# Source one-hots compared in place over their indices, 42 buckets at a time; destination one-hots in a stream of their own

## The chip, the cores and the metric

The kernel runs on one core of one Trainium2 chip. The metric is the device time of one execution in microseconds, as the median of several runs. The core has five engines that matter here: TensorE (PE, with PEld for its weight loads), VectorE (DVE), ScalarE (ACT), GpSimd (POOL) and SyncE (SP), which only issues DMAs in the stage of interest.

## The reference

One GraphSAGE layer over a random graph of N = 12500 nodes with D = 64 features and E = 800000 edges:

```python
nsum = segment_sum(x[src], dst, N)        # add up the features of each node's neighbours
h_neigh = nsum * deg_inv[:, None]
return x @ w_self + h_neigh @ w_neigh
```

`src` and `dst` are uniformly random. The costly part is the gather `x[src]` of 800000 rows and the sum by `dst`.

## The kernel before

Nodes are taken in source blocks of 128 (NB = 98) and destination blocks of 2 x 82 = 164 (NDB = 77). An edge belongs to one of NBID = 77 x 98 = 7546 **buckets** (destination block, source block). The kernel first sorts the edges by bucket, and then computes each bucket with two one-hot matrix products.

*Sorting.* The edges are packed into 32-bit keys, 6250 to a partition, and each partition is sorted by compare-exchange steps on DVE. The sorted runs are cut into three parts (29, 20 and 10 buckets a row), gathered by POOL's indirect DMAs and merged on DVE (`merge_round`, lines 300 to 334). Part 0 is merged before the sums begin; parts 1 and 2 are merged while the sums run, a few DVE steps after every tile, paced by `PACE` (line 52). Decoding a part (`decode_buckets`) writes each bucket's 128 source indices as a row of `sl` in HBM (bf16) and its destination indices into `dlT` in SBUF.

*Summing* (`nodes`, lines 909 to 1055), from about 819 us to 1875 us of the profile. It goes through the buckets in order, in tiles of 8. For each tile:

- `gather` (line 922): for each bucket one matmul on PE (line 932), with the bucket's **source one-hot** (128 x 128, fp16) as weights and the 128 node rows `xh` of its source block as moving data. The result is the gathered features, in `ct` in PSUM (three buffers). One copy of 1024 columns brings them to `xg` in SBUF (six buffers), on ACT (line 942), or on DVE (line 940) in the last part of the stage, for every second tile at which the stock of ready one-hots is nearly down to the next block (line 935).
- `sums` (line 992), two to five tiles later: for each bucket two matmuls of 64 rows (line 1012) with `xg` as weights and the bucket's **destination one-hot** (128 x 82 twice) as moving data, which add into the accumulators of six destination blocks.
- Now and then `extras` and `pick` take edges that did not fit a bucket (lines 955 to 990), and `finish` multiplies with the weights and adds to the output (lines 1070 to 1091).

*The one-hots* come from `one_hots` (line 890), 28 buckets in each step, 270 steps:

- SP issues four DMAs (line 899) that lay the 28 x 128 source indices of the block, broadcast, into all partitions of an index buffer `slb` (three buffers). Each DMA writes every fourth partition.
- DVE compares the buffer with the partition's number into `ohs` (line 901, three buffers): the source one-hots of 28 buckets.
- DVE compares `iota` with the destination indices in `dlT` into `ohd` (line 906, four buffers): the destination one-hots of the same 28 buckets.

`gather` takes a next step of this generator whenever fewer one-hots are ready than the tile needs and 44 more (`AHEAD`, line 66; 36 once parts 1 and 2 are merged). The order of the work is the order of the program: each engine and each DMA queue takes its instructions in the order in which the Python code emits them, and waits at the first whose data or buffer is not free. So DVE's comparisons stand between the merge steps, and SP's loads stand one after another, each waiting until its index buffer is free.

Of the kernel before, what the change touches and what calls it, by code (L numbers as in the profile page):

```python
# [13 lines left out]
BF = mybir.dt.bfloat16  # L14
FH = mybir.dt.float16
I32 = mybir.dt.int32
U32 = mybir.dt.uint32
OP = mybir.AluOpType
# [7 lines left out]
HN = 82  # L26
NDB = -(-N // (2 * HN))
NBID = NDB * NB
# [42 lines left out]
BEHIND = 5e3  # L71
NEARLY = 24
LAG = 4
HELD = 5
OCT = 6
OCTM = 256 // OCT + 1
# [297 lines left out]
class Kernel:  # L374
# [348 lines left out]
    def find_and_gather(self, part, vp):  # L723
# [7 lines left out]
        junk = vp.tile([128, max(n for _, n in WIN.w2[part])], BF, name="junk")  # L731
        for k in range(kpr + LAG):
            if k == 1:
                self.store_rows(part, nc.gpsimd)
            if k < kpr:
                self.count_below(part, k, acc, junk)
            if k >= LAG:
                g = k - LAG
                nc.scalar.activation(ix[:, g:g + 1], acc[:, g:g + 1], AF.Relu, bias=self.c2[part][:, 3, g:g + 1])
# [147 lines left out]
        self.left[part] = (place, s)  # L887
        yield 1

    def one_hots(self, pool):  # L890


        nc = self.nc
        for c in range(0, NBID, 28):
            n = min(28, NBID - c)
            b = pool.tile([128, 28 * 128], BF, name="slb", bufs=3)[:, :n * 128]
            src = self.sl[c:c + n]
            for j in range(4):
                nc.sync.dma_start(b[j::4], bass.AP(tensor=src.tensor, offset=src.offset, ap=[[0, 32], [1, n * 128]]))  # L899
            s = pool.tile([128, 28, 128], FH, name="ohs", bufs=3)[:, :n]  # L900
            nc.vector.tensor_scalar(s.rearrange("p c s -> p (c s)"), b, self.pidx[:, :1], None, op0=OP.is_equal)  # L901
            d = pool.tile([128, 14, HN, 2], FH, name="ohd", bufs=4)[:, :n // 2]
            at = c % TURN
            wide = [128, n // 2, HN, 2]
            ix = self.dlT[:, at:at + n].rearrange("p (c t) -> p c t", t=2)[:, :, None, :].to_broadcast(wide)
            nc.vector.tensor_tensor(d, self.iota[:, None].to_broadcast(wide), ix, op=OP.is_equal)  # L906
            yield [(s[:, j], d[:, j // 2, :, j % 2]) for j in range(n)]

    def nodes(self, pool, aps, mps):


        nc = self.nc
        source = self.one_hots(pool)
        ready = []
        pend = []
        late = []
        done = []
# [4 lines left out]
        def gather(b0, cnt, vector):  # L922

            nonlocal turn
            ct = aps.tile([128, 1024], F32, name="ct", bufs=3)
            ahead = AHEAD - 8 * vector
            while len(ready) < min(cnt + ahead, NBID - b0):
                ready.extend(next(source))
            cols = ready[:cnt]
            del ready[:cnt]  # L930
            for i in reversed(range(cnt)):
                nc.tensor.matmul(ct[:, i * 128:(i + 1) * 128], cols[i][0],  # L932
                                 self.xh[:, (b0 + i) % NB].rearrange("p a f -> p (a f)"), start=True, stop=True)
            xg = pool.tile([128, 1024], FH, name="xg", bufs=6)
            if vector and (len(ready) < min(8 + ahead, NBID - b0 - cnt) or NBID - b0 < 56):
                turn += 1
            else:
                vector = False
            if vector and turn % 2:
                nc.vector.tensor_copy(xg[:, :cnt * 128], ct[:, :cnt * 128])  # L940
            else:
                nc.scalar.activation(xg[:, :cnt * 128], ct[:, :cnt * 128], AF.Copy)  # L942
            return b0, xg, [d for _, d in cols]
# [11 lines left out]
        def pick(b0):  # L955
            if self.picked == len(done) or len([u for u in uses if u[5]]) >= HELD:
                return
            u = next((u for u in uses if not u[5]), None)
            if u and u[1] in self.left and b0 + LEAD >= u[4] * NB:
                _, p, c = u[:3]  # L960
                x = u[5] = pool.tile([128, 128], FH, name="lx", bufs=HELD)
                u[6] = len(done)
                nc.gpsimd.indirect_dma_start(  # L963
                    out=x, out_offset=None, in_=self.xt,
                    in_offset=bass.IndirectOffsetOnAxis(ap=self.left[p][1][:, c:c + 1].bitcast(U32), axis=0))
                self.picked = len(done)

        def spread(u):
            o, p, c, f, e = u[:5]
            u[7] = pool.tile([128, 2, OCT * HN], FH, name="ohl", bufs=HELD)  # L970
            n = slice((f - o * OCT) * HN, (e - o * OCT) * HN)
# [10 lines left out]
        def extras(b0, cnt):  # L982
            o = b0 // (OCT * NB)
            for u in uses[:HELD]:
                if u[5] and not u[7] and len(done) >= u[6] + 10 and b0 + 80 >= (u[4] - 1) * NB:
# [47 lines left out]
        for t, (b0, cnt) in enumerate(tiles):  # L1033
            pend.append(gather(b0, cnt, self.changed))
            if (len(pend) > 5) if self.changed else t % 2:
                while len(pend) > (3 if self.changed else 2):
                    b0 = pend[0][0]
                    if sums(pend.pop(0)):
                        break
                extras(b0, 8)  # L1040
            else:
                pick(b0)
            b0 = tiles[t][0]
            if late and b0 >= late[0][0]:
                if next(late[0][1], self) is self:
                    late.pop(0)
                else:
                    late[0][0] = b0 + 40
            done.append(t)
            yield t  # L1050
# [323 lines left out]
```

## Time and profile before

| what | value |
|---|---|
| median of 3 runs | 1880.74 us (1879.26 to 1881.54) |
| the profiled execution, its time | 1892.56 us |
| the profiled execution, its span | 1890.8 us |
| DVE busy over the span | 1739.8 us (92%) |
| ACT busy | 1125.0 us (59%) |
| PE busy | 969.4 us (51%) |
| POOL busy | 580.3 us (31%) |
| source comparisons, line 901 | 270, 322.9 us on DVE |
| destination comparisons, line 906 | 270, 361.8 us on DVE |
| index loads, line 899 | 1080 DMAs, 224 KB each but the last four |

Times in rows of the profile are in microseconds from the first instruction, unless marked ns. The shares over the whole span mix two very different stages: until about 811 us DVE sorts and PE does nearly nothing; after that all engines work on the sums. Read the stage, not the span. A row of a group has the line, the engine, the operation, what it writes and reads with the shapes, its count, then its busy time and the mean of one, and after a second bar the idle time of the engine ahead of it and who ended it.

### The profile page before, as it was taken

How to read it: one execution, taken by the hardware profiler on the slowest of the kernel's cores; microseconds unless marked ns; L12 is line 12 of the kernel's file. 1: busy time of each engine (PE TensorE's matmuls, PEld its weight loads, DVE VectorE, ACT ScalarE, POOL GpSimd, SP SyncE). 2: the span in 40 equal slices, each digit the busy share in tenths (PEclk: the TensorE clock that was granted, in tenths of full speed). 3: DMA queues.
4: the chain of work that ended last, by engine and by line, in shares of the span. 5: the costliest groups of instructions: out<-in, count | busy, mean ns of one | idle time of the engine just before them, and what ended most of it. 6: DMA issues, size and time to landing. Idle time of an engine off the chain costs nothing.

```text
span 1890.8 us, 54010 instructions
## 1 busy us (share of the span) xinstructions
PE 969.4 (51%) x23335; PEld 850.3 (45%) x23335; DVE 1739.8 (92%) x1728; ACT 1125.0 (59%) x1578; POOL 580.3 (31%) x447
## 2 busy tenths in 40 slices
PE   0042000000000000058878989887888999889996
PEld 0041000000000000047767878776777788678885
DVE  8999999999999999989969999999986999888885
ACT  7281000104001005458979999899898999878875
POOL 2000000045421004404545435473324324432231
PEclk9975555555555555569989999999899999989998
DMA  4353000022001002168969898987797999878884
GB/s 154 70 133 71 0 0 0 37 63 65 14 8 59 22 0 75 51 199 246 285 201 262 274 259 251 294 267 226 217 302 210 275 281 272 274 194 258 262 260 121
DMA packets 176788, 307.77 MB, mean 163 GB/s; under 512 B 127885, under 2 KB 133340, under 8 KB 175772
## 3 DMA queue, kind: packets, MB, share of 16 engines
q1 hardware_dynamic: 98268, 275.58, 44.5%
q0 software_dynamic: 78272, 28.65, 9.5%
q8 instruction: 184, 3.01, 0.6%
q14 instruction: 64, 0.52, 0.1%
HBM read 277.01 MB, written 26.52 MB: 161 GB/s over the span
## 4 chain that ended last, share of the span: by engine, by line
DVE 20%; PE 13%; DMA 11%; issue 9%; ACT 6%; SPq 6%; POOL 1%; DVEq 0%; another core or an unknown queue 0%; POOLq 0%; ACTq 0%
DMA slb<-sl 10%; DVE u L328 7%; PE ct L932 7%; SPq L899 6%; PE acc L1012 5%; ACT xg L942 4%; DVE ohs L901 4%; DVE ohd L906 4%; DVE u L362 2%; DVE u L316 1%; PE po L1079 1%; ACT u L689 0%; PE acc L980 0%; ACT junkb L544 0%; POOL out L1088 0%
## 5 line engine op out<-in xcount | busy, mean ns | idle before, releaser
L942 ACT ACTIVATE xg<-ct 128x1024 f16<-128x1024 f32 x918 | 863.3, 1061 | 124.8 <-PE ct L932 88.3
L932 PE MATMUL ct<-xh,ohs 128*128 128x128 f16 x7546 | 537.9, 224 | 86.7 <-DVE ohs L901 48.9
L932 PEld LDWEIGHTS <-ohs 128*128 128x128 f16 x7546 | 453.2, 100 | 126.3 <-DVE ohs L901 55.4
L328 DVE TENSOR_TENSOR u<-u 128x1512 f32<-128x1512 f32 (+57 forms) x316 | 426.8, 1361 | 13.0 <-ACT u L312 8.3
L1012 PE MATMUL acc<-ohd,xg 64*128 64x82 f16 x15092 | 401.3, 202 | 50.3 <-ACT xg L942 21.3
L963 POOL DMA_INDIRECT lx<-xt,ls x127 | 240.4, 1893 | 458.3 <-PE acc L980 377.3
L1012 PEld LDWEIGHTS <-xg 64*128 64x128 f16 x15092 | 327.9, 97 | 111.1 <-issue 39.7
L901 DVE TENSOR_SCALAR ohs<-slb,pidx 128x3584 f16<-128x3584 bf16 x270 | 322.9, 1196 | 54.2 <-PE ct L932 19.5
L906 DVE TENSOR_TENSOR ohd<-iota,dlT 128x2296 f16<-128x2296 bf16 x270 | 361.8, 1340 | 0.9 <-PE acc L1012 0.9
L500 PE MATMUL stp<-cx,swapa 128*128 128x16 f32 (+1 forms) x12 | 3.1, 335 | 445.9 <-DVE swapa L496 445.9
L500 PEld LDWEIGHTS stp<-cx,swapa 128*128 128x128 f32 x12 | 2.6, 274 | 446.4 <-issue 236.4
L260 DVE TENSOR_TENSOR a<-b 128x1040 f32<-128x1040 f32 (+41 forms) x130 | 194.8, 1539 | 5.2 <-ACT b L262 2.1
L260 DVE TENSOR_TENSOR b<-a 128x1040 f32<-128x1040 f32 (+46 forms) x150 | 194.7, 1346 | 3.4 <-DVE a L260 0.5
L529 POOL DMA_INDIRECT u<-d,ixa x48 | 72.5, 1510 | 402.1 <-ACT junka L517 346.7
L1088 POOL DMA_DIRECT2D out<-o x27 | 100.1, 3835 | 93.4 <-ACT o L1082 76.2
L312 ACT ACTIVATE u<-u 128x256 f32<-128x256 f32 (+14 forms) x60 | 33.0, 623 | 160.4 <-DVE u L316 124.3
L778 PE MATMUL tr<-idb,l 128*128 128x128 bf16 x59 | 7.8, 268 | 188.8 <-ACT l L772 188.8
L262 ACT ACTIVATE b<-a 128x2 f32<-128x2 f32 (+31 forms) x41 | 16.0, 405 | 147.8 <-DVE a L260 131.1
L778 PEld LDWEIGHTS <-l 128*128 128x128 bf16 x59 | 4.4, 116 | 191.2 <-ACT l L772 190.8
L316 DVE TENSOR_TENSOR u<-u 128x2016 f32<-128x2016 f32 (+11 forms) x40 | 62.5, 1574 | 25.5 <-DMA lx<-xt,ls 15.7
L262 ACT ACTIVATE a<-b 128x1 f32<-128x1 f32 (+24 forms) x34 | 8.6, 259 | 119.4 <-DVE b L260 114.7
L556 POOL DMA_INDIRECT u<-da,ixb x24 | 36.5, 1519 | 79.8 <-ACT ixb L504 75.8
(151 smaller groups left out, 821.1 us busy)
## 6 DMA issues: line engine op xcount, KB each, us to landing
slb<-sl SPq DMA_DIRECT2D x1076, 224.0 KB
xt<-xh SPq DMA_DIRECT2D x1, 3136.0 KB
out<-o POOLq DMA_DIRECT2D x25, 123.0 KB
own<-os SPq DMA_DIRECT2D x12, 256.0 KB
out<-os SPq DMA_DIRECT2D x12, 256.0 KB
rd<-dst SPq DMA_DIRECT2D x4, 521.0 KB
rs<-src SPq DMA_DIRECT2D x4, 521.0 KB
lx<-xt,ls POOLq DMA_INDIRECT x127
```

The lines of the kernel that those rows point to most:

```text
L260: nc.vector.tensor_tensor(view(dst, lo + sh, [[st, g], [1, l]]), x, y, op=op)
L316: nc.vector.tensor_tensor(at(oth, to, n), x, y, op=op)
L328: nc.vector.tensor_tensor(to, at(cur, ln + lo, n), at(cur, lo + k, n), op=op)
L529: nc.gpsimd.indirect_dma_start(out=u[:, i * w:(i + 1) * w], out_offset=None, in_=src, in_offset=bass.IndirectOffsetOnAxis(ap=self.start[pa ...
L899: nc.sync.dma_start(b[j::4], bass.AP(tensor=src.tensor, offset=src.offset, ap=[[0, 32], [1, n * 128]]))
L901: nc.vector.tensor_scalar(s.rearrange("p c s -> p (c s)"), b, self.pidx[:, :1], None, op0=OP.is_equal)
L906: nc.vector.tensor_tensor(d, self.iota[:, None].to_broadcast(wide), ix, op=OP.is_equal)
L932: nc.tensor.matmul(ct[:, i * 128:(i + 1) * 128], cols[i][0], self.xh[:, (b0 + i) % NB].rearrange("p a f -> p (a f)"), start=True, stop=True)
L942: nc.scalar.activation(xg[:, :cnt * 128], ct[:, :cnt * 128], AF.Copy)
L963: nc.gpsimd.indirect_dma_start(out=x, out_offset=None, in_=self.xt, in_offset=bass.IndirectOffsetOnAxis(ap=self.left[p][1][:, c:c + 1].bit ...
L1012: nc.tensor.matmul(acc[h][:, db % OCT * HN:(db % OCT + 1) * HN], xg[r, i * 128:(i + 1) * 128], d[r], start=db % OCT == 0 and sb == 0, stop ...
L1088: nc.gpsimd.dma_start(out, o[:n, at], accum_op=OP.add)
```

## The change

`one_hots` is split into two generators.

`source_hots` makes the source one-hots of 42 buckets in each step (`SCH`), 180 steps. It has one kind of buffer, of which there are four: SP's four DMAs load the broadcast indices into it, and DVE's comparison writes the fp16 one-hots over the bf16 indices, element by element. The buffer is free again when PE's matmuls have used its last bucket.

`dest_hots` makes the destination one-hots of 28 buckets in each step (`DCH`), with the same operation and the same four buffers as before.

`gather` keeps two stocks, `ready` for the source and `spare` for the destination one-hots, and steps the generator whose stock is smaller until both hold what the tile needs and `AHEAD` more.

```diff
+SCH = 42
+DCH = 28
...
-    def one_hots(self, pool):
+    def source_hots(self, pool):
         nc = self.nc
-        for c in range(0, NBID, 28):
-            n = min(28, NBID - c)
-            b = pool.tile([128, 28 * 128], BF, name="slb", bufs=3)[:, :n * 128]
+        for c in range(0, NBID, SCH):
+            n = min(SCH, NBID - c)
+            b = pool.tile([128, SCH * 128], BF, name="ohs", bufs=4)[:, :n * 128]
             src = self.sl[c:c + n]
             for j in range(4):
                 nc.sync.dma_start(b[j::4], bass.AP(tensor=src.tensor, offset=src.offset, ap=[[0, 32], [1, n * 128]]))
-            s = pool.tile([128, 28, 128], FH, name="ohs", bufs=3)[:, :n]
-            nc.vector.tensor_scalar(s.rearrange("p c s -> p (c s)"), b, self.pidx[:, :1], None, op0=OP.is_equal)
-            d = pool.tile([128, 14, HN, 2], FH, name="ohd", bufs=4)[:, :n // 2]
+            s = b.bitcast(FH)
+            nc.vector.tensor_scalar(s, b, self.pidx[:, :1], None, op0=OP.is_equal)
+            yield [s[:, j * 128:(j + 1) * 128] for j in range(n)]
+
+    def dest_hots(self, pool):
+        nc = self.nc
+        for c in range(0, NBID, DCH):
+            n = min(DCH, NBID - c)
+            d = pool.tile([128, DCH // 2, HN, 2], FH, name="ohd", bufs=4)[:, :n // 2]
...
             nc.vector.tensor_tensor(d, self.iota[:, None].to_broadcast(wide), ix, op=OP.is_equal)
-            yield [(s[:, j], d[:, j // 2, :, j % 2]) for j in range(n)]
+            yield [d[:, j // 2, :, j % 2] for j in range(n)]
...
-            while len(ready) < min(cnt + ahead, NBID - b0):
-                ready.extend(next(source))
-            cols = ready[:cnt]
+            need = min(cnt + ahead, NBID - b0)
+            while min(len(ready), len(spare)) < need:
+                if len(ready) <= len(spare):
+                    ready.extend(next(sources))
+                else:
+                    spare.extend(next(dests))
+            cols = list(zip(ready[:cnt], spare[:cnt]))
             del ready[:cnt]
+            del spare[:cnt]
```

More of the change, by code (lines that the diff above doesn't have):

```diff
@@ L906, in one_hots @@
             nc.vector.tensor_tensor(d, self.iota[:, None].to_broadcast(wide), ix, op=OP.is_equal)
-            yield [(s[:, j], d[:, j // 2, :, j % 2]) for j in range(n)]
+            yield [d[:, j // 2, :, j % 2] for j in range(n)]
     def nodes(self, pool, aps, mps):
         nc = self.nc
-        source = self.one_hots(pool)
-        ready = []
+        sources, dests = self.source_hots(pool), self.dest_hots(pool)
+        ready, spare = [], []
         pend = []
```

## The prediction

> **What bounds the kernel now.** The change touches one stage, so I first looked for the engine that sets its pace: the view of busy time by stretch, over the summing stage (819 to 1875 us) cut at its quiet places. Columns: length, then busy time and instructions of PE, PEld, DVE, ACT, POOL, then granted clock, DMA share, GB/s.
>
> ```profile
> 819.00:1400.00 581.00, 503.57 (x12464) 440.64 (x12465) 550.68 (x673) 521.87 (x669) 261.53 (x141) 0.95 0.84 255
> ...
> 1460.00:1560.00 100.00, 90.74 (x2384) 79.85 (x2380) 97.61 (x107) 94.35 (x115) 32.28 (x13) 1.00 0.91 281
> 1560.00:1875.00 315.00, 280.43 (x7107) 250.03 (x7103) 270.63 (x330) 261.10 (x328) 102.09 (x62) 0.95 0.83 245
> ```
>
> and over two pieces of it:
>
> ```profile
> 1010.00:1260.00 250.00, 223.41 (x5709) 195.45 (x5707) 248.23 (x268) 232.24 (x293) 125.03 (x57) 0.99 0.88 265
> 1640.00:1875.00 235.00, 207.41 (x5313) 186.75 (x5312) 198.91 (x238) 186.88 (x230) 65.33 (x39) 0.95 0.80 234
> ```
>
> DVE is full in the first and third stretch (95% and 98%; 99% in 1010 to 1260), where it also merges runs. PE and ACT follow at 87 to 94%, so little can be won before they bind. In the last stretch DVE is at 86%, PE at 89%: there PE, not DVE, is nearest to the bound.
>
> Next, the chain of waits in 1000 to 1260, for what releases DVE, and three of its pieces from 1110 on (start, us, what):
>
> ```profile
> by line: DMA slb<-sl 32.4%; SPq L899 13.3%; DVE ohs L901 10.5%; DVE ohd L906 8.7%; issue 8.4%; PE ct L932 8.4%; DVE u L328 7.9%; PE acc L1012 7.0%; ACT xg L942 1.5%; DVE ohl L972 1.0%; PE po L1079 0.7%; PE acc L980 0.6%; DVEq L901 0.4%; ACT
> ...
> 1110.19 6.56 DMA slb<-sl
> ...
> 1118.06 0.45 SPq L899
> ...
> 1120.45 4.86 DMA slb<-sl
> ```
>
> This is a loop: comparing a block frees its index buffer, SP issues four loads into it (1118.06 to 1120.45, 2.4 us), the last lands 4.9 to 6.6 us later, and three blocks on that buffer is compared. It takes 45.7% of that chain, yet the idle time it leaves is small, as the waits of 819 to 1400 (first two rows) and of 1400 to 1875 (the last) show (us, times, longest):
>
> ```profile
> PE ct L932 <- DVE ohs L901: 45.0, 21, 22.1
> ...
> DVE ohs L901 <- DMA slb<-sl: 11.3, 7, 6.3
> ...
> DVE ohs L901 <- DMA slb<-sl: 7.3, 6, 2.2
> ```
>
> So the loop ends just as DVE comes free: DVE and the loop are both near critical, and DVE's own work is the larger.
>
> **The change, part by part.** The 28-bucket comparisons, 270 of them, become 180 of 42 (7546 = 179 x 42 + 28). Only their fixed cost goes. Two timeline rows from mid-stage and two from the end price it (the first number is the start):
>
> ```profile
> 1120.60 1.15 DVE L901 TENSOR_SCALAR ohs<-slb,pidx 128x3584 f16<-128x3584 bf16 x1
> 1121.66 1.35 DVE L906 TENSOR_TENSOR ohd<-iota,dlT 128x2296 f16<-128x2296 bf16 x1
> ...
> 1868.42 0.68 DVE L901 TENSOR_SCALAR ohs<-slb,pidx 128x1792 f16<-128x1792 bf16 x1
> 1869.01 0.75 DVE L906 TENSOR_TENSOR ohd<-iota,dlT 128x1148 f16<-128x1148 bf16 x1
> ```
>
> Durations overlap, so starts are compared: 28 buckets hold DVE 1.06 us, 14 hold it 0.59 us. Fourteen buckets cost 0.47 us, and the fixed part is 2 x 0.59 - 1.06 = 0.12 us. A block of 42 holds it 1.53 us. Before: 269 x 1.06 + 0.59 = 285.7 us; after: 179 x 1.53 + 1.06 = 274.9; saved 10.8 us. Where does it count? Line 901 by stretch (only DVE busy):
>
> ```profile
> 819.00:1400.00 581.00, 174.95 (x147) 0.95 0.84 255
> ...
> 1460.00:1560.00 100.00, 34.93 (x29) 1.00 0.91 281
> ```
>
> Of the 147 + 29 = 176 comparisons in the two full stretches a third goes: 59 x 0.12 = **7.1 us** on the path. The other 3.7 us lie in stretches where PE's matmuls hide them.
>
> [...]
>
> Comparing in place: no row has this operation at its four-elements rate. The nearest are an in-place integer operation and two made alike, one in place and one not:
>
> ```profile
> L761 DVE TENSOR_SCALAR v<-v 128x512 int32<-128x512 int32 x14 | 6.0, 427 | 0.5
> ...
> L453 DVE SCALAR_TENSOR_TENSOR g<-g,a 128x1042 int32<-128x1042 int32 x4 | 5.0, 1246 | 0.1
> L455 DVE SCALAR_TENSOR_TENSOR a<-rs,s 128x1042 int32<-128x1042 int32 x4 | 5.0, 1245 | 0.4
> ```
>
> In place 1246 ns, otherwise 1245: I take zero. The other end is that the operation falls to half rate, 180 x 1.4 us = 252 us more DVE work; a rival below. A gain has no reason: the elements stay the same.
>
> Comparisons held up by POOL: some overlap a POOL write and last twice as long.
>
> ```profile
> 1162.78 4.21 POOL L1088 DMA_DIRECT2D out<-o  x1
> ...
> 1163.42 2.29 DVE L901 TENSOR_SCALAR ohs<-slb,pidx 128x3584 f16<-128x3584 bf16 x1
> ```
>
> ```profile
> L901 DVE TENSOR_SCALAR ohs<-slb,pidx 128x3584 f16<-128x3584 bf16 x269 | 322.3, 1198 | 54.2 <-PE ct L932 19.5 <-DMA slb<-sl 18.6 <-issue 6.4
> ```
>
> The mean of 1198 is 48 ns over the 1.15 us of the undisturbed row above, 13 us in all. Fewer operations may meet POOL less often (a third less, 4.3 us won) or longer ones more often (half more, 6.5 us lost). I take zero, since POOL's work stays as it is.
>
> Buffers and loads: three index and three one-hot buffers of 28 become four shared ones of 42, 168 buckets either way. Loads fall from 1080 to 720, bytes stay, so the DMA engines (84% busy) gain nothing sure. SP now waits for the ct matmuls of the block four before instead of for DVE. Behind that wait stand only the next such loads, and DVE waits for them. With one bucket in about 1.05/8 = 0.131 us (250 us over 5709/24 = 238 tiles), the lead works out so. Before: from one comparison to that three blocks on, 84 buckets, 11.0 us, against 1.06 + 2.4 of issues + 4.86 = 8.3. After: loads start when PE finishes a block, at bucket 42k, for the comparison that stands in the program 44 to 52 buckets ahead of 42(k + 3): 74 to 82 buckets, 9.7 to 10.7 us, against 2.4 + 4.86 = 7.3 if the larger load lands as fast, 2.4 + 7.3 = 9.7 if its landing grows with its bytes. So the loop is met, barely at worst, and a DVE that falls behind now gives the loads more time instead of delaying them. Of the 11.3 us, 6.3 are the start; of the other 5.0 I count half as gone: **2.5 us**, bounds 0 and 5.0.
>
> [...]
>
> The start: PE's first matmul waits for the first block.
>
> ```profile
> 813.31 36.97 SPq L899 DMA_DIRECT2D slb<-sl  x42
> ...
> 819.53 1.15 DVE L901 TENSOR_SCALAR ohs<-slb,pidx 128x3584 f16<-128x3584 bf16 x1 [6.34 <-DMA slb<-sl]
> ```
>
> Of these 6.2 us, 2.3 are issues; the remaining 3.9 grow by 0 to 2, I take 1.5, and the comparison by 0.47: **2.0 us lost**. PE then has 42 buckets where it had 28.
>
> Destination one-hots: same 270 operations, four buffers, only the place in DVE's order differs; nothing. DVE casts of xg:
>
> ```profile
> L940 DVE CAST xg<-ct 128x1024 f16<-128x1024 f32 x32 | 39.0, 1220 | 20.4 <-PE ct L932 18.8 <-ACT o L1082 1.0 <-issue 0.5
> ```
>
> Line 935 picks them when a new source block is near, now every 42 buckets: about ten move to ACT, 11 us of work where ACT has 187 of 235 us; PE covers it, and uncovered it would cost at most those 11. Part 2's rows are now read from bucket 6258 on, not 6272. At 1640, after the part is written, PE still has 5313/24 = 221 tiles, so stands near bucket 5775, some 60 us ahead: nothing.
>
> Sum: -7.1 - 2.5 + 2.0 = **-7.6 us**. The profiled execution took 1892.56 us (span 1890.8) and would take 1885.0; the median of the runs, 1880.74, was 11.8 lower, and I carry the difference over: **1873 us**. Its own range, from no loop gain and the slow start (-4.6) to all 5.0, a quick start and fewer collisions (-16), is 1865 to 1877.
>
> **Rivals.** *The loop was the real bound.* For it: its 45.7% of the chain. Against it: DVE is idle so little. Then PE's waits for one-hots beyond the start, 45.0 - 22.1 = 22.9 us, go: -22.9 + 2.0, **1860 us**. *PE and ACT take over at once.* For it: ACT at 94% in the fullest stretch and PE at 91%. Then the 7.1 falls away, and 2.0 lost stands against 2.5: **1880 us**. *The loads come late (slower).* They now wait for PE, and a load like that of 6.56 us, half as large again, lands after 2.4 + 9.8 = 12.2 us, 2.0 beyond the mean lead of 10.2; DVE stands, and with it the destination one-hots, merges and casts queued behind. It decides where landing exceeds some 7.8 us after the last issue. The 12 waits after the start (6 in each half of the stage) each grow by 2.0; the six of the first half, where DVE is full, cost 12.0, against 7.1 won and 2.0 lost: +6.9, **1888 us**. *In place is slower:* DVE gets 252 us; its idle time in the three stretches, 30 + 2 + 44 = 76 us, takes some, so about +170, **2050 us**.
>
> **How the numbers follow.** Forecast 0.45, loop 0.15, no change 0.20, late loads 0.17, slow in place 0.03. A measurement tells 0.2%, 3.8 us: faster 0.45 + 0.15 = 0.60, same 0.20, slower 0.17 + 0.03 = 0.20. The range reaches from just below the loop case, 1858, to just beyond the late loads, 1889; outside are slow in place and the far halves of these two, about 0.18.
>
> **What would show it.** Right: line 901's successor 180 times, start to start 1.53 us; DVE busy 11 us lower; 720 loads; SP waiting for PE; waits of the comparison for slb under 12 us after the start. Wrong: comparisons near 3 us (in place), slb waits above 25 us (late loads), or DVE idle growing by as much as it was relieved (PE and ACT bind).

## The result, and the profile after

| | before | after |
|---|---|---|
| median of 8 runs | 1881.70 us (1878.69 to 1885.12) | 1901.83 us (1890.02 to 1910.88) |
| the profiled execution, time / span | 1892.56 / 1890.8 us | 1905.11 / 1903.4 us |

The ratio after to before is 1.0103, with a 95% interval of 1.0078 to 1.0127: about 20 us slower, where 8 us faster was forecast. The runs after also spread more, over 21 us instead of 6.

First the busy time by stretch in the kernel after (columns as in the prediction: length, busy time and instructions of PE, PEld, DVE, ACT, POOL, granted clock, DMA share, GB/s).

```profile
819.00:1400.00 581.00, 495.63 (x12306) 437.65 (x12307) 539.45 (x622) 513.52 (x653) 262.61 (x139) 0.95 0.78 253
1460.00:1560.00 100.00, 93.00 (x2417) 82.69 (x2415) 93.48 (x94) 95.14 (x115) 39.23 (x13) 0.98 0.81 262
1560.00:1875.00 315.00, 273.26 (x6995) 243.84 (x6993) 255.57 (x295) 269.62 (x338) 104.42 (x63) 0.97 0.81 254
```

In the third stretch DVE is down from 97.61 to 93.48 us of 100, so it is relieved. But in the first, PE executes 12306 matmuls instead of 12464 at the same clock, and DVE, which needs less time for each bucket, idles 41.6 us instead of 30.3. The time went somewhere that is neither engine's work.

The comparison itself does what was said of it. The first row is its group in the list of costly groups, the second is from the view of the tile `ohs` (duration in ns as least, median and longest).

```profile
L903 DVE TENSOR_SCALAR ohs<-ohs,pidx 128x5376 f16<-128x5376 bf16 x180 | 299.3, 1663 | 26.1 <-DMA ohs<-sl 26.1
```

```profile
L903 DVE TENSOR_SCALAR ohs<-ohs,pidx x180: 1148/1614/2951, 821.1 to 1878.8; 128x5376 f16<-128x5376 bf16 x179, 128x3584 f16<-128x3584 bf16 x1
```

One of 42 buckets lasts 1614 ns, 0.46 us more than the 1.15 us of one of 28. In the timeline it holds DVE 1.52 us from its start to the next:

```profile
1040.88 1.61 DVE L903 TENSOR_SCALAR ohs<-ohs,pidx 128x5376 f16<-128x5376 bf16 x1
1042.40 0.25 DVE L987 TENSOR_SCALAR ohl<-wide,lp 128x164 f16<-128x164 f16 x1
```

Next, what PE waits for from 819 to 1890 (what it was about to do, what it waited for, us in all, times, longest), before and then after.

```profile
PE ct L932 <- DVE ohs L901: 48.9, 26, 22.1
PE acc L1012 <- ACT xg L942: 21.3, 18, 4.3
PE acc L1012 <- issue: 20.7, 40, 2.0
PE ct L932 <- issue: 17.4, 33, 1.5
```

```profile
PE ct L947 <- DVE ohs L903: 51.5, 10, 24.2
PE acc L1027 <- issue: 42.5, 44, 2.6
PE ct L947 <- issue: 21.9, 21, 2.5
PE acc L1027 <- ACT xg L957: 19.2, 15, 4.5
```

The waits for one-hots and for ACT stay about as they were. What grows is "issue", time in which PE waited for nothing that the profile shows: 38.9 us before (with a row of 0.8 that is not shown) and 64.4 after, 25.5 us more. The profiled execution grew by 12.6 us in all, so this more than covers what was lost; a part of it is made up elsewhere.

The chain of waits of 1400 to 1885, before and after, tells the same:

```profile
by line: issue 18.9%; DMA slb<-sl 15.3%; PE ct L932 12.9%; SPq L899 11.8%; PE acc L1012 9.8%; ACT xg L942 9.8%; DVE ohs L901 5.3%; DVE ohd L906 3.9%; POOL out L1088 1.6%; PE po L1079 1.5%; another core or an unknown queue 1.2%; DVE xg L940 
```

```profile
by line: PE ct L947 28.2%; PE acc L1027 21.0%; issue 18.0%; ACT xg L957 11.9%; POOL u L558 2.2%; DMA u<-da,ixb 1.9%; DMA ohs<-sl 1.9%; PE acc L995 1.6%; DVE ohs L903 1.6%; DVE ohd L916 1.6%; POOL out L1103 1.5%; PE po L1094 1.3%; DMA sl<-l 
```

The loop of loads and comparisons, 27.1% there before, has gone but for 1.9%. PE's matmuls and issue make up two thirds of it now. So PE took over in this part of the stage, and time that PE loses there lengthens it.

What PE waits for can be read off its timeline (start, duration, matmuls, and in brackets the idle time ahead):

```profile
891.86 0.68 PE L947 MATMUL ct<-xh,ohs 128*128 128x128 f16 x9 [2.04 <-issue]
892.47 0.80 PE L1027 MATMUL acc<-ohd,xg 64*128 64x82 f16 x32
893.20 1.07 PE L947 MATMUL ct<-xh,ohs 128*128 128x128 f16 x16
894.20 0.80 PE L1027 MATMUL acc<-ohd,xg 64*128 64x82 f16 x32
894.93 1.07 PE L947 MATMUL ct<-xh,ohs 128*128 128x128 f16 x16
895.93 0.60 PE L1027 MATMUL acc<-ohd,xg 64*128 64x82 f16 x22
896.68 0.37 PE L1027 MATMUL acc<-ohd,xg 64*128 64x82 f16 x10 [0.15 <-issue]
...
902.10 0.75 PE L1027 MATMUL acc<-ohd,xg 64*128 64x82 f16 x29 [0.27 <-issue]
...
908.33 1.77 PE L947 MATMUL ct<-xh,ohs 128*128 128x128 f16 x16 [1.95 <-issue]
```

From the gap at 891.86 to that at 896.68 are 9 + 32 + 16 + 32 + 16 + 22 = 127 matmuls; the stretches to 902.10 and to 908.33 hold 127 each, too. Each matmul has a weight load, so a gap comes after 254 PE instructions. Beside it, from the page after: the instructions of PE, and the queue that the profiler calls "instruction" (packets, MB, share).

```profile
PE 966.7 (51%) x23335; PEld 853.9 (45%) x23335; DVE 1712.0 (90%) x1629; ACT 1131.6 (59%) x1587; POOL 592.1 (31%) x447
```

```profile
q8 instruction: 186, 3.05, 0.6%
```

3.05 MB in 186 packets are 16.4 KB each, and 46670 instructions of PE in 186 packets are 251 each, about one packet to such a stretch. In the trace's own DMA records, all 63 issue gaps of over 0.2 us (64.2 us) end 1.2 to 1.6 us after a packet of this queue has ended. From these numbers I read the gaps so: **PE runs out of instructions and waits for the next fetch**, and the profile lists these fetches as a DMA queue beside that of the index loads.

Counted by place, the growth is larger than that of "issue". With the records of PE and its sequencer counted in order, all 65 issue gaps after (64.5 us with the smallest) lie a multiple of 256 records apart, to within two: they stand at the border of a block of 256. Before, only 28 of 75 gaps do (21.1 us); the other 47 (17.9 us) lie inside blocks. So **late fetches grew from 21 to 64 us**. The gaps inside blocks seem to go with the chip and not with the kernel. The traces of e5 to e8 and e13 to e16 below, from two chips, have none; those of e1 to e4, e9 to e12, e17 and e18, from three others, have 14 to 28 us each. The kernel before takes 1876 and 1877 us on those two chips, 1889 to 1890 us on these three. What these gaps are, and which chips the profiles before and after came from, is not known.

Of some 180 packets of this queue in the stage, 63 are followed by a gap of over 0.2 us, 64.2 us of PE's idle time in all; the other two thirds leave none of that size.

Where PE loses no more to issue than before, the change pays. The ct matmuls alone (one a bucket) in two stretches, PE and PEld, before and then after:

```profile
1010.00:1060.00 50.00, 26.29 (x384) 21.85 (x381) 1.00 0.91 269
1110.00:1260.00 150.00, 77.21 (x1108) 64.53 (x1109) 0.99 0.88 269
```

```profile
1010.00:1060.00 50.00, 23.99 (x334) 20.42 (x335) 0.93 0.77 238
1110.00:1260.00 150.00, 79.30 (x1168) 67.03 (x1166) 1.00 0.87 281
```

In 1110 to 1260, where PE has 6.6 us of issue after and 8.2 before, the kernel after does 5% more buckets. In 1010 to 1060, with 6.6 us of issue where there was none (and a granted clock of 0.93 instead of 1.00), it does 13% fewer. A gain shows in the one stretch, and is lost again in the other.

### The profile page after: what moved, and what is told of

Its sections match the earlier page's. It is cut to its first block, busy times and chain, and to the rows that moved or that the text cites. A ratio compares the mean times of both kernels' runs of the same rounds, so it can differ in the third digit from the quotient of the medians.

```text
span 1903.4 us, 53639 instructions
## 1 busy us (share of the span) xinstructions
PE 966.7 (51%) x23335; PEld 853.9 (45%) x23335; DVE 1712.0 (90%) x1629; ACT 1131.6 (59%) x1587; POOL 592.1 (31%) x447
## 3 DMA queue, kind: packets, MB, share of 16 engines
q8 instruction: 186, 3.05, 0.6%
## 5 line engine op out<-in xcount | busy, mean ns | idle before, releaser
L978 POOL DMA_INDIRECT lx<-xt,ls x127 | 246.0, 1937 | 482.1 <-PE acc L995 408.1
L916 DVE TENSOR_TENSOR ohd<-iota,dlT 128x2296 f16<-128x2296 bf16 x270 | 361.8, 1344 | 25.0 <-PE acc L1027 24.8
L903 DVE TENSOR_SCALAR ohs<-ohs,pidx 128x5376 f16<-128x5376 bf16 x180 | 299.3, 1663 | 26.1 <-DMA ohs<-sl 26.1
L531 POOL DMA_INDIRECT u<-d,ixa x48 | 72.5, 1510 | 402.1 <-ACT junka L519 346.8
L955 DVE CAST xg<-ct 128x1024 f16<-128x1024 f32 (+1 forms) x23 | 27.2, 1188 | 44.5 <-PE ct L947 44.5
```

The source lines that it names most:

```text
L531: nc.gpsimd.indirect_dma_start(out=u[:, i * w:(i + 1) * w], out_offset=None, in_=src, in_offset=bass.IndirectOffsetOnAxis(ap=self.start[pa ...
L903: nc.vector.tensor_scalar(s, b, self.pidx[:, :1], None, op0=OP.is_equal)
L978: nc.gpsimd.indirect_dma_start(out=x, out_offset=None, in_=self.xt, in_offset=bass.IndirectOffsetOnAxis(ap=self.left[p][1][:, c:c + 1].bit ...
```

## The experiments

What DVE waits for after, from 819 to 1890, raises two suspicions of its own:

```profile
DVE ohs L903 <- DMA ohs<-sl: 26.1, 11, 7.9
DVE ohd L916 <- PE acc L1027: 24.8, 19, 3.5
```

The theories, with the letters that the expectations use for some of them: PE's instruction **fetches** are delayed by the index loads; **C**, the separate stream of destination one-hots costs the time (DVE now waits 24.8 us at `ohd` for PE, 0.9 before); **L**, the loads come late; **P**, the larger packets (10752 bytes, before 7168) do it; **K**, buffers released by PE instead of DVE; **G**, too much loaded in one burst. (In the expectations A and F are the fetches, B is L, and Q is a fetch that waits behind all load bytes outstanding.) "Issue" below is PE's issue time from 819 us on, in the one profiled run of each kernel, and "late" the part of it at block borders (after: 64.4 and 64; before: 38.9 and 21). Beside them stands DVE's wait for loads at the comparison (26.1 us in the kernel after, 18.6 before). Each ratio is to the kernel before, measured on the same chip.

**e1: the streams alone.** Index and one-hot buffers as before (28 buckets, three and three), two generators.

```diff
-SCH = 42
+SCH = 28
...
-            b = pool.tile([128, SCH * 128], BF, name="ohs", bufs=4)[:, :n * 128]
+            b = pool.tile([128, SCH * 128], BF, name="slb", bufs=3)[:, :n * 128]
...
-            s = b.bitcast(FH)
+            s = pool.tile([128, SCH * 128], FH, name="ohs", bufs=3)[:, :n * 128]
```

> Only the split into two streams is kept: 28 buckets a comparison, three index buffers and three one-hot buffers as before. A (PE runs out of instructions: its fetches stand behind the larger loads): PE idle with nothing to wait for stays near the 39 us of before (64 after the change), time within 0.4% of before. B (loads late because they wait for PE): as before as well, since loads wait for DVE again. C (the separate stream makes DVE stand at destination one-hots whose buffers PE still holds, 24.8 us after the change against 0.9): DVE stands there for over 15 us, and the time is 10 to 20 us over before.

Ratio 0.9992 [0.9972, 1.0013], issue 36.0, late 17. The stream by itself costs nothing that can be measured.

**e2 and e3: in place with other sizes,** six buffers of 28 (shown) and four of 36 (`SCH = 36`, `bufs=4`).

```diff
-SCH = 42
+SCH = 28
...
-            b = pool.tile([128, SCH * 128], BF, name="ohs", bufs=4)[:, :n * 128]
+            b = pool.tile([128, SCH * 128], BF, name="ohs", bufs=6)[:, :n * 128]
```

> The change with blocks of 28 in six shared buffers: the same 168 buckets of buffer, in place, loads wait for PE, the smaller block. A: the unit of load is that of before, so PE's idle time without a releaser falls back to about 40 us and the time to 1875 to 1887 us, although DVE's fixed costs are not saved. B: loads still wait for PE, with a longer lead (140 buckets ahead instead of 126), so DVE's waits for loads fall below the 26 us of the changed kernel, PE's idle time without a releaser stays near 64 us, and the time stays over 1892. C: still 1895 to 1905, with DVE standing at destination one-hots for 25 us.

> The change with blocks of 36 in four buffers: smaller load, shorter lead (108 buckets instead of 126). A: PE's idle time without a releaser lies between those of before and after (45 to 58 us), and the time below the changed kernel's, 1885 to 1897. B: the lead of 108 less 44 to 52 buckets is 7.3 to 8.4 us against 2.4 + 6.2 for a load, so DVE waits for loads for over 45 us (26 after the change), and the time is over 1905. C: 1895 to 1905.

28 x 6: 1.0025 [0.9992, 1.0057], issue 47.9, late 27, loads 14.5. 36 x 4: 1.0175 [1.0135, 1.0215], issue 84.9, late 70, loads 54.2. So in-place buffers of 28 lose little, if anything, and 36 is worse than 42; the loss doesn't simply grow with the block.

**e4: a quarter of the index bytes.** After the first four blocks each load brings a quarter of its columns; the comparison works on what the buffer holds, so that the one-hots and the sums are not those of the reference. Here and in e9, e13, e14 and e16 to e18 the shared buffers are tiles that are held for the whole stage (lines not shown).

```diff
...
+            m = n * 128 if c < 4 * SCH else n * 32
...
-                nc.sync.dma_start(b[j::4], bass.AP(tensor=src.tensor, offset=src.offset, ap=[[0, 32], [1, n * 128]]))
+                nc.sync.dma_start(b[j::4, :m], bass.AP(tensor=src.tensor, offset=src.offset, ap=[[0, 32], [1, m]]))
```

> The changed kernel, in which every load after the first four blocks brings only the first quarter of its columns; the rest of a block keeps old values, so the one-hots and the sums made from them are left wrong, while every instruction of the engines stays. It takes away three quarters of the load bytes. A: PE's idle time without a releaser falls from 64 to under 20 us, and the time to 1850 to 1872. B: DVE's waits for loads (26 us) vanish but for the start, PE's idle time without a releaser stays near 64, the time falls by at most 15 us to about 1888. C: DVE still stands at destination one-hots for some 25 us, and the time stays near 1900.

0.9793 [0.9753, 0.9833], 1853.71 against 1889.45 us, issue 24.8, late 5. DVE's wait at `ohd` rose to 28.4 us in this fastest of all kernels, so that wait (C) isn't what costs the time. With fewer bytes the changed program is far faster than the kernel before. That could be fetches, or loads that come early (L); e9 separates the two.

**e9: e4 and the other three quarters beside it,** as a load that nobody waits for, into HBM (so these bytes are also written there). Against e4:

```diff
+            if c >= 4 * SCH:
+                idle = self.dram.tile([128, SCH * 96], BF, name="idle", bufs=8)
+                nc.sync.dma_start(idle[:, :n * 96], bass.AP(tensor=src.tensor, offset=src.offset + n * 32,
+                                                            ap=[[0, 128], [1, n * 96]]))
```

> The run with quarter loads (output left wrong in the same way), plus one more DMA for each block that copies the other three quarters' bytes to a place in HBM which nobody reads or waits for. The load bytes are back in the DMA queues, but DVE waits only for the first quarter. F (PE's instruction fetches are held up by load bytes in the queues, and that is what costs): PE's idle time without a releaser goes from 24.8 back to over 50 us and the ratio from 0.979 to 1.000 or more. L (what costs is that the loads land late for DVE): the ratio stays under 0.988, whatever that idle time does.

1.0249 [1.0212, 1.0286], 1935.94 against 1890.3 us. PE's waits in e4 and then in e9, and DVE's for loads in e9:

```profile
PE acc L1031 <- issue: 13.1, 32, 1.0
PE ct L951 <- issue: 11.2, 22, 2.4
```

```profile
PE acc L1035 <- issue: 53.3, 69, 2.5
PE ct L955 <- issue: 39.0, 40, 2.9
...
PE ct L955 <- DVE ohs L911: 6.6, 4, 2.6
```

```profile
DVE ohs L911 <- DMA ohs<-sl: 7.7, 1, 7.7
```

The bytes that nobody uses cost over 80 us. DVE waits for a load once, at the start, and PE hardly for one-hots; PE's issue time rises from 24.8 to 92.3, and late fetches from 5 to 73. That is not L. The other 19 us of issue are of the kind inside blocks, which e4 has too.

**e5, e6, e7, e8: smaller pieces.** The buffer gets a small space after every 14 (or 7) buckets, so that a row of it is written in pieces of 3584 (1792) bytes: e5 and e6 are the kernel after with 14 and 7, e7 the kernel before with 14, e8 is e2 with 14. For e5:

```diff
-            b = pool.tile([128, SCH * 128], BF, name="ohs", bufs=4)[:, :n * 128]
+            b = pool.tile([128, SCH // 14, 14 * 128 + 4], BF, name="ohs", bufs=4)[:, :n // 14, :14 * 128]
...
-                nc.sync.dma_start(b[j::4], bass.AP(tensor=src.tensor, offset=src.offset, ap=[[0, 32], [1, n * 128]]))
+                nc.sync.dma_start(b[j::4], bass.AP(tensor=src.tensor, offset=src.offset,
+                                                   ap=[[0, 32], [14 * 128, n // 14], [1, 14 * 128]]))
...
```

> The changed kernel with each partition's load cut into three packets of 14 buckets (3584 B instead of 10752 B): a gap of four elements between them in the buffer keeps them apart; same bytes, same 720 issues, same order. P (an instruction fetch of PE waits its turn behind single load packets, so the delay goes with the packet's size): PE's idle time without a releaser falls from 64 to under 38 us, and the ratio to before from 1.010 to below 1.000. Q (a fetch waits behind all load bytes outstanding): it stays at 55 to 70 us, ratio 1.005 to 1.015. B (loads late because they wait for PE's blocks): 55 to 70 us as well, DVE's waits for loads stay at 26 us, ratio 1.005 to 1.015.

> As the run before with six packets of 7 buckets (1792 B). P: PE's idle time without a releaser at 30 us or less, ratio 0.99 to 1.00, unless the many packets make the loads land later (then DVE's waits for loads go over 30 us). Q and B: 55 to 70 us, ratio 1.005 to 1.015.

> The kernel before with two packets of 3584 B for each partition instead of one of 7168 B, nothing else. P: its own idle time of PE without a releaser, 38 us, falls to under 30, and the time by 5 to 12 us (ratio 0.994 to 0.998). Q: 35 to 42 us, ratio 0.998 to 1.002. B: the same as Q.

> Six shared buffers of 28, in place, with packets of 3584 B. P: PE's idle time without a releaser falls from 48 to about 30 us, ratio from 1.0025 to 0.992 to 0.999. Q and B: 45 to 50 us, ratio 1.000 to 1.005.

| | ratio | issue, all of it late, us | loads, us |
|---|---|---|---|
| e5 | 1.0308 [1.0263, 1.0352] | 53.1 | 13.9 |
| e6 | 1.0162 [1.0119, 1.0204] | 71.7 | 39.9 |
| e7 | 1.0002 [0.9978, 1.0025] | 15.2 | 24.3 |
| e8 | 1.0030 [1.0000, 1.0059] | 26.8 | 4.0 |

e5 can't be read as meant. Its comparison became slower, and with it DVE:

```profile
L904 DVE TENSOR_SCALAR ohs<-ohs,pidx x180: 1148/2076/3014, 821.4 to 1896.3; 128x5376 f16<-128x5376 bf16 x179, 128x3584 f16<-128x3584 bf16 x1
```

Three pieces take 2076 ns where six (e6) and one take 1614. Issue falls with pieces of 3584 bytes in all three pairs (64.4 to 53.1, 38.9 to 15.2, 47.9 to 26.8), but much of that is the idle time inside blocks, which no trace of this chip has. Late fetches fall by 11 us in e5, whose DVE is slower, by 6 in e7 (21 to 15) and not at all in e8 (27 to 27); with 1792 bytes they rise to 72. Small pieces are no cure, and P fails. In e7 the 6 us less win no time that can be measured.

**e10, e11, e12: shapes of the buffers.** Eight shared buffers of 21 (`SCH = 21`, `bufs=8`), three of 56 (`SCH = 56`, `bufs=3`), and (e11, shown) 42 buckets in two index and two one-hot buffers, not in place, so that DVE releases the index buffers.

```diff
-            b = pool.tile([128, SCH * 128], BF, name="ohs", bufs=4)[:, :n * 128]
+            b = pool.tile([128, SCH * 128], BF, name="slb", bufs=2)[:, :n * 128]
...
-            s = b.bitcast(FH)
+            s = pool.tile([128, SCH * 128], FH, name="ohs", bufs=2)[:, :n * 128]
```

> The change with blocks of 21 in eight buffers: 168 buckets again, loads released by PE again, half the bytes in each burst of loads, lead 147 buckets, 360 comparisons. F with the burst's size as its cause: PE's idle time without a releaser under 40 us (48 with 28, 64 with 42). K (loads released by PE's own blocks fall in step with PE's fetches): 55 us or more. L: DVE's waits for loads under 10 us after the start. Ratio 0.998 to 1.006, of which some 0.5% are the 90 comparisons more than with 28.

> Blocks of 42, not in place: two index buffers and two one-hot buffers, the same memory; loads are released by DVE as before the change. F by burst size: PE's idle time without a releaser 55 us or more, as with 42 in place. K: 45 us or less. L: a load is released by the comparison two blocks before, 84 buckets or 11 us of lead as before the change, for 9 us of a larger load: DVE waits 20 to 40 us for loads and also for PE; ratio 1.01 to 1.03.

> Blocks of 56 in three buffers: 168 buckets, loads released by PE, a lead of 112 buckets, bursts a third larger than with 42. F by burst size: PE's idle time without a releaser over 80 us. L: 112 less 44 to 52 buckets are 8 to 9 us against about 10 for a load: DVE waits over 60 us. Both: ratio 1.02 to 1.05; which of the two grows tells them apart.

e11: 1.0158 [1.0112, 1.0205], issue 72.5, late 56. In-place work and PE's release of the index buffers aren't needed for late fetches, which speaks against K; the time isn't clean, since with two one-hot buffers DVE also waits 68.7 us for PE to free one. e12: 1.0371 [1.0329, 1.0414], issue 109.4, late 96, and loads 113.4, so fetches and late loads together. e10: 1.0287 [1.0254, 1.0321], with issue of only 34.1, late 6. Here another wait took over:

```profile
DVE ohs L903 <- DMA ohs<-sl: 93.7, 74, 5.5
```

```profile
L901 SPq DMA_DIRECT2D ohs<-sl x1440: 447/592/2688, 813.6 to 1923.2; - x180
```

1440 loads at 592 ns are 852 us of SP's time in a stage of some 1100, and SP's waits for other engines and for DMAs before a load add up to some 125 us, where they are some 550 in the kernel after: the loads come late mainly because SP is nearly always issuing.

**e13 and e14: loads that cover all 128 partitions.** e13 loads a block of 42 in three DMAs of 14 buckets, each of which waits only for its own 14 buckets in PE; e14 in one (as in the diff of e15, with 42).

```diff
-            for j in range(4):
-                nc.sync.dma_start(b[j::4], bass.AP(tensor=src.tensor, offset=src.offset, ap=[[0, 32], [1, n * 128]]))
+            for lo in range(0, n, 14):
+                m = min(14, n - lo) * 128
+                nc.sync.dma_start(b[:, lo * 128:lo * 128 + m], bass.AP(
+                    tensor=src.tensor, offset=src.offset + lo * 128, ap=[[0, 128], [1, m]]))
```

> The changed kernel, comparisons of 42 in place in four buffers, but the load of a block comes in three DMAs of 14 buckets for all 128 partitions (instead of four DMAs of 42 buckets for every fourth partition), each released when PE has used its own 14 buckets. Same bytes, bursts a third as large (459 KB instead of 1376). G (what costs is PE's instruction fetches queued behind the burst of load bytes): PE's idle time without a releaser falls from 64 to under 45 us, and the ratio to at most 1.000, 0.990 to 1.000, since the relief of DVE stays. L (loads late): the last third is released no earlier than the block is now, with less to bring; DVE's waits for loads fall under 15 us. If that idle time falls and the ratio stays at 1.010, G is wrong about the cost.

> Control for the run before: the changed kernel with the load of a block as one DMA of 42 buckets for all 128 partitions, released by the whole block. The burst is as large as in the changed kernel, only the number of DMAs falls from four to one. G: PE's idle time without a releaser 55 us or more, ratio 1.005 to 1.020. If it were the number of DMAs that matters, that idle time would fall as in the run before.

e13: 1.0054 [1.0027, 1.0081], issue 45.8, loads 7.6 (7.3 of it the start). e14: 1.0133 [1.0104, 1.0162], issue 64.2, loads 23.2. All of this issue is late. It looked as if the burst (G) decided.

**e15: the kernel before with one load a block.** All else as before: 28 buckets, DVE's comparisons, DVE's release, the one stream.

```diff
-            for j in range(4):
-                nc.sync.dma_start(b[j::4], bass.AP(tensor=src.tensor, offset=src.offset, ap=[[0, 32], [1, n * 128]]))
+            nc.sync.dma_start(b, bass.AP(tensor=src.tensor, offset=src.offset, ap=[[0, 128], [1, n * 128]]))
```

> The kernel before with one DMA of 28 buckets for all 128 partitions instead of four for every fourth partition. The burst of 917 KB stays but is issued at once. G: PE's idle time without a releaser as before, 30 to 45 us, ratio 0.996 to 1.004. The loop of comparison, issue and landing loses the 2 us of issues, so DVE's waits for loads may fall from 12 us after the start to under 8.

1.0111 [1.0071, 1.0151]: a loss as large as that of the change, from the pattern of the loads alone, though the pattern isn't that of the change. PE's waits and DVE's:

```profile
PE ct L931 <- DVE ohs L900: 45.0, 13, 21.0
PE acc L1011 <- issue: 35.6, 32, 2.9
PE ct L931 <- issue: 26.9, 20, 3.5
```

```profile
DVE ohs L900 <- DMA slb<-sl: 9.1, 6, 5.2
```

Loads are less late than before (9.1 us against 18.6), PE waits less for one-hots (45.0 against 48.9), a partition's row has its old 7168 bytes, and issue is 64.3 instead of 38.9 us, late fetches 64 instead of 21. All 52 issue gaps over 0.2 us end 1.2 to 1.7 us after a fetch. None of L, P, K and C is at work here, so none is needed for such a loss.

**e16, e17, e18: the burst theory tried.** e16 is e13 with six buffers of 28; e17 has six DMAs of 7 buckets for each 42; e18 has two DMAs for each 14, of every second partition (shown against e13).

```diff
-                nc.sync.dma_start(b[:, lo * 128:lo * 128 + m], bass.AP(
-                    tensor=src.tensor, offset=src.offset + lo * 128, ap=[[0, 128], [1, m]]))
+                for j in range(2):
+                    nc.sync.dma_start(b[j::2, lo * 128:lo * 128 + m], bass.AP(
+                        tensor=src.tensor, offset=src.offset + lo * 128, ap=[[0, 64], [1, m]]))
```

> Comparisons of 28 in place in six buffers with loads of 14 buckets for all partitions, each released by its own 14 buckets. G: the same bursts of 459 KB as in the run with 42, so PE's idle time without a releaser is the same within 8 us, and the ratio some 0.3 to 0.6% above that of 42, by the fixed cost of 90 more comparisons where DVE is full; 0.995 to 1.004.

> Comparisons of 42 in place in four buffers, loads in six DMAs of 7 buckets for all partitions (230 KB), each released by PE's own 7 buckets, about 0.95 us apart, so that the load bytes follow PE at 240 GB/s instead of coming 1376 KB at a time. G: PE's idle time without a releaser at 40 us or less, ratio 0.992 to 1.001. If the number or the small packets of the DMAs hold fetches up instead, it stays at 46 us or more and the ratio at 1.005 or above.

> Comparisons of 42 in place, loads in six DMAs of 14 buckets for every second partition (230 KB), two for each 14 buckets that PE has used; strided issues take SP 0.59 us instead of 0.32, so SP cannot put more than 390 GB/s into the queues, as with the 224 KB loads of the kernel before. G: PE's idle time without a releaser 45 us or less, below the 45.8 of the run with three DMAs of 459 KB, ratio 0.993 to 1.003.

e16: 1.0124 [1.0098, 1.0150], issue 57.5, all of it late, loads 0.2. e17: 1.0108 [1.0071, 1.0146], issue 62.6, late 44. e18: 1.0037 [1.0012, 1.0063], issue 61.5, late 41. Bursts half as large as in e13 (e17) leave as many late fetches (44 us against 46) and more time, and e16 has the bursts of e13 but neither its late fetches nor its time: G in this form is wrong. e18 is nearly as fast as the kernel before although its issue is high; it has 20 us of the kind inside blocks, like the other kernel on its chip (e17, 18 us), and no more late fetches than e13.

**All together.** Ordered by late fetches, the ratios are: 15 to 27 us, 0.999 to 1.003 (e7, e1, the kernel before with 21, e8, e2); 41 to 46, 1.004 to 1.011 (e18, e13, e17); 58 to 64, 1.010 to 1.013 (e16, e14, e15 and the change itself); 70 and 72, 1.0175 and 1.016 (e3, e6); 73, 1.025 (e9); 96, 1.037 (e12). Outside stand e5, e10 and e11 (56, 1.016), each with a slower part of its own in its rows, and e4 (5), which moves fewer bytes. The late fetches are those of one execution, while the runs of one kernel lie up to 28 us apart, so neighbours in this order can't be told apart. No kernel that does all the work was measurably faster than the one before.

## Why the prediction was wrong

- **The comparison**: right. 1.52 us from start to start, 1.53 forecast; in place it costs nothing (1614 ns, against 1616 in e11, which writes another buffer). 14 buckets more (1792 elements a partition) take 469 ns more, 1614 against the 1145 of one of 28 before: 3.8 elements a ns, which is as far as any run shows the prediction's "four-elements rate". DVE is busy 1712.0 us instead of 1739.8, of which nine casts that went to ACT (32 to 23; about ten were forecast) are a part. In the stretch 1110 to 1260, with no more issue than before, PE does 5% more buckets.
- **The step that failed** is "Loads fall from 1080 to 720, bytes stay, so the DMA engines (84% busy) gain nothing sure". It counted DVE as the only one that waits for these engines and so priced a new cut of the same bytes at zero, never below it. PE waits for DMAs too, by the gaps at block borders for its instructions; that wait, in "issue" with 38.9 us, was in the waits of before, and the prediction has no term for it. It grew by 25.5 us, and late fetches in it from 21 to 64. e15 shows that another cut of the same bytes alone can do this, at 1.0111. For the change's own cut, e1 (its stream alone, 0.9992) and e2 (in place, loads of 28, 1.0025) leave the block of 42.
- **"The loads come late"** had the sign and not the mechanism. DVE's waits for loads are 26.1 us, just above the 25 that the forecast gave for it; without the start, 7.9 us, they are 18.2, against 18.6 - 6.3 = 12.3 before, so where 2.5 us of waiting were to go, some 6 came. But with these waits cut to 9.1 (e15) or to 7.7 (e9) the loss stays. They add to it in e3, e10 and e12.
- **"PE and ACT take over at once"** was half right. PE did take over, as the chain shows, and ACT's part in it is little changed (9.8% to 11.9%). The case was priced at 1880 by letting DVE's 7.1 us fall away and leaving PE's idle time as it was; PE, which took over, brought its own waits, and they got longer (issue 38.9 to 64.4 us). "DVE idle growing" was named as the sign of it, and it grew (30.3 to 41.6 us up to 1400).
- **The start**: the first comparison begins at 821.1 instead of 819.53, and PE's first wait grew from 22.1 to 24.2 us; 2.0 was forecast.
- **The destination stream**: nothing, as forecast (e1).

**What stays open** is which property of the loads delays a fetch. By my own reading of the DMA records a fetch's packet lasts 1.0 us on average in every kernel; what differs is when it starts. The mean delay, from the earliest point in PE's program at which a fetch was ever seen to start, went from about 2.4 to 3.3 us, and the share over 4 us from 8% to 32%; e15 has 3.3 us and 35%, e4 1.3 us and 2%. Packets, bursts, number of DMAs and who releases the buffers each fail as the single answer: four strided loads of 28 are good in e1 and fair in e2; 36 is worse than 42; e16 has the loads of e13 and more late fetches. Nor is the share of time for which the DMA engines are busy the answer, since it fell from 0.84 to 0.78 (819 to 1400) while fetches got later. How the 43 us of late fetches become 20 us of time is not worked out piece by piece, and the idle time inside blocks has no explanation.

## What to carry to other kernels

When PE takes over from another engine, look at its "issue" idle first: if the gaps stand one instruction block or several apart (here 127 matmuls each), late fetches are the first suspect, and a change to bulk DMAs can be a change to PE as well (e15: 64 us of late fetches, 21 before). Count the gaps at block borders apart from the others, which here seem to go with the chip. Price a new cut of the same bytes with a loss as its one end, never with zero. Test it by changing only the loads in the old kernel, as in e15, before anything else is rebuilt.

## What the runs showed of the hardware

- PE's idle time at borders of its blocks of 256 records was 6 (e10) to 96 us (e12) in kernels with the same matmuls and the same load bytes; with nothing but the index loads changed it was 64 us (e15), 21 before.
- An in-place comparison from bf16 to fp16 of 5376 elements took as long (1614 ns) as one that writes another buffer (1616, e11); cut into three equal pieces with a small space between, it took 2076 (e5), in six 1614 (e6).
- SP took 592 ns (median; before, after and e10) to issue a load of every fourth partition and 320 ns (e13) for one of all 128 with 14 buckets:

```profile
L905 SPq DMA_DIRECT2D ohs<-sl x539: 319/320/1620, 813.4 to 1851.7; - x180
```
